# Pacing the convolution steps by a running account of VectorE's open work

## The chip, the cores and the metric

The kernel runs on one core of a Trainium2 chip. The metric is the device time of one execution in microseconds; of the kernel before, three runs took 519.13, 519.4 and 521.94 us, so the median is 519.4. The profile is of a further execution of 519.61 us, with a span of 517.8 us and a mean granted TensorE clock of 0.997.

## What is computed

The reference is a transformer block with adaptive layer norm: a gated long convolution over 2048 tokens, then a gated feed-forward layer. Cut to what matters, with D = 576 channels, S = 2048 tokens and F = 4608 hidden units:

```python
mod = silu(c) @ w_mod                      # six rows of D: sa, ca, ga, sb, cb, gb
h = layernorm(x) * (1 + ca) + sa
k_shift = causal_4_tap_filter(A_k, shift_k)
kv = k_shift * A_v
y = irfft(rfft(kv, 2 * S) * rfft(ssm_k, 2 * S))[:S] + kv * ssm_D   # causal convolution along tokens
x = x + ga * (h * y)
h = layernorm(x) * (1 + cb) + sb
out = x + gb * ((silu(h @ w1) * (h @ w3)) @ w2)
```

All inputs are bf16. The feed-forward layer of a token needs the convolution at that token, and the convolution at a token needs all tokens before it.

## The kernel before

**Two kinds of work.** The tokens are cut into 8 blocks of 256 for the convolution and into 4 row blocks of 512 (two blocks each) for the feed-forward layer. The feed-forward layer is nearly all TensorE work. The convolution is mostly VectorE work: for each block TensorE makes the spectra X (of kv) and W (of the filter) with small DFT matmuls, VectorE forms V from two neighbouring W, and then multiplies and adds a pair X[i], V[s-i] for every earlier block i (`pair`: products of 128 x 3456 elements, lines 414, 420, 422). VectorE makes the real parts (`real_parts`), TensorE transforms back (`inverse`, L554), VectorE gates the result and adds it to x (`residual`, L568 and L569), then the second layer norm follows and the rows are transposed on TensorE (L586) and evicted by ScalarE into h2T (L616), the operand of the feed-forward matmuls. Block 1's norm ends with L483 on VectorE; blocks 2 to 7 take sums on ScalarE (L452), then L458, L459 on VectorE, a power on GpSimd (L460), L466 on VectorE, and the rows on ScalarE (L581).

**How they are interleaved.** The convolution of the *next* row block runs beside the feed-forward layer of the present one. Block 0 is done alone at the start (`first_block`, to about 34 us). Row block 0 then starts with the tokens of block 0 alone (24 hidden chunks of 128, 256 tokens wide, two chunks to an item) while `conv_second` makes block 1; then come the tokens of block 1 for the same chunks and all 512 tokens for the rest, while `conv(2)` makes blocks 2 and 3. Row blocks 1 and 2 run beside `conv(4)` and `conv(6)`; row block 3 has no convolution beside it and its own loop (`stream_halves`).

A row block has two parts. `stream` computes silu(h w1) * (h w3): per item 16 or 8 full matmuls (L949) and a few over the last 64 channels (L960) into a PSUM tile of two banks, silu on ScalarE (L968), a copy of the other half on ScalarE (L970), and one product on VectorE (L971, called "product" below, 36 to a row block counting all 512 tokens). Products write `h3`. There are 4 PSUM tiles for everything, and 4 buffers for the copies. `down` then multiplies `h3` by w2 (L1061) in two halves of 288 columns, 144 matmuls each; after each half VectorE scales and adds the result (L1078, L1079). After the sixth of nine chunks of the second half, the program calls `end()` and `turn_all`, so that the transpose of the last block for the next row block stands there.

**What sets the order.** The convolution is written as generators. Each step lays out some instructions and yields a cost in microseconds of VectorE time. A negative yield says that the chain now waits for another engine for that long; `mix` fills such a wait with steps of a second generator, and if that has run out, it yields the wait as a positive cost. The feed-forward loops call `advance` after each item and after each down chunk, and `advance` lays out convolution steps. Before, `advance(cost)` adds a fixed amount to what is due and lays out steps until their costs have used it up. The amount is a rate times TensorE's time: 1.8 in the first stage (RATE1), then CONV_US of the row block over a stage time, times HEAD_PACE (1.8) for the first 8 items of row blocks 1 and 2; `conv(2)` starts with 12 us due. This is the order of layout; a scheduler of the layer underneath takes it as a priority and fixes the order in which the instructions of each engine are queued, by dependences and free buffers. Loads go through one queue, SyncE's, in its own order: weights for w1 and w3 into three buffers `wst` (two of them alternate in row blocks 1 to 3), w2 chunks, k and v rows, and the spectra of old blocks, which are spilled to DRAM and read back (`keep_x`, `keep_v`, `get`).

Of the kernel before, what the change touches and what calls it, by code (L numbers as in the profile page):

```python
# [26 lines left out]
NW13 = 3  # L27
W2C = 4
NW2 = 4
CONV_US = (72.0, 97.0, 108.0)  # L30
RATE1 = 1.8
FIRST_DUE = 12.0
N1 = 24
SPLIT = 2
HEAD = 8
HEAD_PACE = 1.8
EPS = 1e-5
EARLY_GETS = 6

# [7 lines left out]
class _Kernel:  # L47
    def __init__(self, ctx, tc, q, k, v, shift_k, ssm_k, ssm_D, w1, w3, w2, c, w_mod, out):
        self.tc, self.nc = tc, tc.nc
        self.q, self.k, self.v = q, k, v  # L50
        self.shift_k, self.ssm_k, self.ssm_D = shift_k, ssm_k, ssm_D
        self.w1, self.w3, self.w2, self.c, self.w_mod, self.out = w1, w3, w2, c, w_mod, out
        pool = lambda name, **kw: ctx.enter_context(tc.tile_pool(name=name, **kw))
        self.const = pool("const", bufs=1)
        self.psum = pool("psum", bufs=4, space=bass.MemoryType.PSUM)
        self.dram = pool("spill", bufs=1, space=bass.MemoryType.DRAM)
        self.spec = pool("spec", bufs=4)
        self.wprev = pool("wprev", bufs=2)
        self.prod = pool("prod", bufs=1)
        self.acc = pool("acc", bufs=1)  # L60
        self.ld = pool("ld", bufs=1)
        self.kvp = pool("kvp", bufs=1)
        self.x1p = pool("x1p", bufs=4)
        self.lnp = pool("lnp", bufs=1)
        self.small = pool("small", bufs=4)
        self.hp = pool("hp", bufs=4)
        self.xo, self.hg, self.accs, self.l1 = {}, {}, {}, {}
        self.X, self.V, self.Wl = {}, {}, {}
        self.w13, self.kept = {}, {}
        self.gets = 0  # L70

    def ps(self, shape=(P, 2, 512), dtype=F32):
        return self.psum.tile(list(shape), dtype, name="ps", tag="ps")
# [272 lines left out]
        yield 0.75  # L346

    def x_spectrum(self, s):
        X = self.spec.tile([P, 6, D], BF16, name="X", tag="X", bufs=3)
        self.X[s] = X  # L350
        if s < SPLIT:
            yield from self.forward(self.Fb, self.kv, lambda e, cs: X[:, 3 * e + 1 + cs, :])
        else:
            yield from self.forward2(self.Fb, self.kv, X[:, 1:3, :], X[:, 0:4:3, :], X[:, 4:6, :])

    def x_sums(self, s):
        X = self.X[s]
        self.nc.vector.tensor_add(X[:, 0:6:3, :], X[:, 1:6:3, :], X[:, 2:6:3, :])
        if 3 < s < NBLK - 2:
            self.keep_x(s)  # L360
        yield 0.75
# [538 lines left out]
            nc.sync.dma_start(t[:, 5 * i:5 * i + 4, :], w[0:512, cols].rearrange("(a p) f -> p a f", p=P))  # L900
            nc.sync.dma_start(t[64 * i:64 * i + 64, 4, :], w[512:D, cols])

    def advance(self, cost):

        self.due += cost
        while self.due > 0 and self.steps is not None:
            c = next(self.steps, None)
            if c is None:
                self.steps = None
                break  # L910
            self.due -= c
            self.spent += c

    def stream(self, r, jobs, rate, size, finish=False):

        nc = self.nc  # L920
        hT = self.h2T[r % 2]
        items = []
        for job in jobs:
            m = RB // (job[2] - job[1])
            items += [(job, fi, m) for fi in range(0, FC, m)]
        gus, ws = {}, {}

        def load(job):
            fc, _, _, buf, also = job
            if fc not in self.w13 and buf is not None:  # L930
                if r == 0:
                    with self.behind(nc.sync):
                        self.load_w13(fc, buf)
                else:
                    self.load_w13(fc, buf)
            w = self.kept[fc] = self.w13.pop(fc) if buf is not None else self.kept[fc]
            ws[job[0:3]] = w
            if also is not None:
                with self.behind(nc.sync):
                    also()  # L940


        def full(k, first):
            (fc, t0, t1, _, _), fi, m = items[k]
            w, n = ws[fc, t0, t1], t1 - t0
            for a in range(m):
                for i in range(2):
                    for ct in range(4):
                        nc.tensor.matmul(gus[k][:, i, a * n:(a + 1) * n],  # L949
                                         w[:, 5 * i + ct, (fi + a) * P:(fi + a + 1) * P], hT[:, ct, t0:t1],  # L950
                                         start=(first and ct == 0 and a == 0),
                                         stop=(not first and ct == 3 and a == m - 1))

        def rest(k, first):
            (fc, t0, t1, _, _), fi, m = items[k]
            w, n = ws[fc, t0, t1], t1 - t0
            for a in range(m):
                for i in range(2):
                    rows = slice(64 * i, 64 * i + 64)
                    nc.tensor.matmul(gus[k][:, i, a * n:(a + 1) * n],  # L960
                                     w[rows, 4, (fi + a) * P:(fi + a + 1) * P], hT[rows, 4, t0:t1],
                                     start=(first and a == 0), stop=(not first and a == m - 1))

        def hide(k):
            (fc, t0, t1, _, _), fi, m = items[k]
            f = fc * FC + fi
            h3 = self.h3[:, f:f + m, t0:t1]
            nc.scalar.activation(h3, gus[k][:, 0, :].rearrange("p (a t) -> p a t", a=m), ACT.Silu)  # L968
            u = self.hp.tile([P, RB], BF16, name="u", tag="u")
            nc.scalar.copy(u[:], gus[k][:, 1, :])  # L970
            nc.vector.tensor_mul(h3, h3, u[:].rearrange("p (a t) -> p a t", a=m))  # L971
            del gus[k]
            self.advance(rate * 2.05 * (HEAD_PACE if r > 0 and k < HEAD else 1.0))

        def begin(k):
            if items[k][1] == 0:
                load(items[k][0])
            gus[k] = self.ps()
        for k in range(0, len(items), size):
            early, late = range(k, k + size // 2), range(k + size // 2, k + size)  # L980
            for m in early:
                begin(m)
                full(m, True)
            for m in early:
                rest(m, False)
            for m in late:
                begin(m)
                rest(m, True)
            for m in early:
                hide(m)  # L990
            if finish and late.stop == len(items):
                self.end()
            for m in late:
                full(m, False)
                hide(m)
# [44 lines left out]
                part(f - 1, 1)  # L1040
                hide(f - 1)

    def down(self, r, rate):
        nc = self.nc
        for h in range(2):

# [3 lines left out]
            for f0 in range(0, NF, W2C):  # L1050
# [17 lines left out]
                if (f0 // W2C) % 4 == 3:  # L1068

                    leave = ((self.keep_v, 3), (self.keep_v, 2), (self.keep_x, 2), (self.keep_x, 3)) if r == 0 else ()  # L1070
                    for keep, i in leave[2 * h + f0 // (4 * W2C):][0:1]:
                        keep(i)
                self.advance(rate * W2C * 4 * 0.126)
            for t in range(4):
                s, cc = 2 * r + t // 2, t % 2
                x1 = self.xo[s]
# [7 lines left out]
                    nc.sync.dma_start(self.out[B * s:B * (s + 1), :].rearrange("(p c) d -> p c d", c=2),  # L1084
                                      x1[:])

    def begin(self, steps, due=0.0):
        self.steps, self.due, self.spent = steps, due, 0.0

    def end(self):  # L1090
        self.advance(1e9)

    def run(self):
        self.setup()
        self.early_loads()
        last = self.first_block()

        n1 = N1 // FC
        with self.tc.issue_after(last):
            self.begin(self.conv_second())  # L1100
            self.stream(0, [(fc, 0, 256, fc % 2, self.block_two if fc == n1 - 1 else None) for fc in range(n1)],
                        RATE1, 2, finish=True)
            self.end()
        sync = self.nc.sync.engine
        last = self.in_order(0, [sync])[sync]
        with self.tc.issue_after(last):
            self.row_blocks(n1)
# [6 lines left out]

    def row_blocks(self, n1):
        for r in range(NRB):
            cost = 0
            if r + 1 < NRB:
                s0 = 2 * r + 2

                self.begin(self.conv(s0), FIRST_DUE if r == 0 else 0.0)
                cost = CONV_US[r]
            time = 110.0 * 0.85 - (N1 * 1.03 if r == 0 else 0)
            rate = cost / time
            if r == 0:

                jobs = [(fc, 256, 512, None, None) for fc in (n1 - 2, n1 - 1)]
# [6 lines left out]
            else:  # L1134
                spills = {1: (self.keep_x, 1), 2: (self.keep_v, 0), 4: (self.keep_v, 1)} if r == 1 else {}
                jobs = [(fc, 0, RB, (r + fc) % 2, (lambda f, i: lambda: f(i))(*spills[fc]) if fc in spills else None)
                        for fc in range(NF // FC)]
            if r == NRB - 1:
                self.stream_halves(r)
            else:  # L1140
                self.stream(r, jobs, rate, 2)
            self.down(r, rate)
            self.end()


# [51 lines left out]
```

## Time and profile before

| quantity | value |
|---|---|
| median of 3 runs | 519.4 us |
| span of the profiled run | 517.8 us |
| TensorE matmul busy | 498.4 us (96%) |
| VectorE busy | 345.5 us (67%) |
| ScalarE busy | 292.9 us (57%) |
| products of spectra, L420 and L422 | 28 each, 54.6 us each |
| product of the stream, L971 | 108, 44.5 us |
| row block 0 starts (first L949) | 34.28 us |
| transpose of block 1 (L586) | 65.38 us |
| row block 1 starts | 171.45 us |
| row block 2 starts | 292.1 us |
| row block 3 starts | 408.57 us |

A row of the profile's groups names the source line, the engine, the operation, the tiles out and in, the shapes and the number of instructions, then the busy time and the mean duration of one, then the idle time of that engine just before them and what ended it. "PE" is TensorE's matmuls, "DVE" VectorE, "ACT" ScalarE, "POOL" GpSimd, "SP" SyncE. Busy time of TensorE includes pipelining, so two neighbouring matmuls overlap in the records; the time from the start of one to the start of the next is the better price. The slices give the busy share of each fortieth of the span in tenths.

### The profile page before, as it was taken

What the parts mean: (1) busy time and instruction counts of PE and PEld (TensorE: products, weight loads), DVE (VectorE), ACT (ScalarE), POOL (GpSimd) and SP (SyncE); (2) the same over time, 40 slices, a digit from 0 to 9 for tenths busy, and PEclk for the clock granted to TensorE, in tenths of its full rate; (3) what the DMA queues carried; (4) which work ended last, traced back from release to release, by engine and by line L of the source; (5) the groups of instructions that cost most, each with busy time, mean ns of one, the idle gap of its engine ahead of it and who ended that gap; (6) DMA issues with size and microseconds to landing.
All of it is one profiled execution on the core that took longest, in us unless ns stands there. A gap on an engine that the chain in (4) does not pass through costs nothing.

```text
span 517.8 us, 9255 instructions
## 1 busy us (share of the span) xinstructions
PE 498.4 (96%) x3650; PEld 294.8 (57%) x3650; DVE 345.5 (67%) x557; ACT 292.9 (57%) x581; POOL 26.1 (5%) x75
## 2 busy tenths in 40 slices
PE   7999989889989999899999999999999999999997
PEld 3667765456868544343677644434587644444775
DVE  8888799999997287989999637998711222221012
ACT  5748689649254488577641467958651355555000
POOL 3100000000000001000001000000100000000000
PEclk9999999989999999999999999999999999999999
DMA  8947959646998696688788549653655535532462
GB/s 262 331 151 210 308 178 289 203 143 221 315 342 270 207 312 230 214 284 289 230 270 280 161 147 361 200 173 91 184 147 151 161 107 176 175 110 77 117 181 69
DMA packets 102207, 107.80 MB, mean 208 GB/s; under 512 B 5075, under 2 KB 94228, under 8 KB 102164
## 3 DMA queue, kind: packets, MB, share of 16 engines
q1 hardware_dynamic: 102142, 107.21, 66.5%
q8 instruction: 28, 0.46, 0.4%
q14 instruction: 15, 0.12, 0.1%
q10 hardware_dynamic: 22, 0.01, 0.0%
HBM read 96.00 MB, written 11.21 MB: 207 GB/s over the span
## 4 chain that ended last, share of the span: by engine, by line
PE 70%; DVE 20%; DMA 4%; ACT 3%; issue 2%; POOL 1%; SPq 0%; DVEq 0%; POOLq 0%; ACTq 0%
PE ps L949 24%; PE ps L1061 22%; PE ps L1016 14%; PE ps L960 4%; DVE p L420 3%; DMA wst<-in_B_w_dram 3%; DVE z L422 3%; DVE h L971 2%; PE ps L318 2%; DVE z L414 1%; DVE kv L342 1%; DVE kvt L341 1%; PE ps L253 1%; DMA knat<-in_A_ssm_k_dram 1%; ACT junk L452 1%
## 5 line engine op out<-in xcount | busy, mean ns | idle before, releaser
L949 PE MATMUL ps<-h2T,wst 128*128 128x512 bf16 (+1 forms) x1056 | 201.1, 341 | 1.9 <-DMA wst<-in_B_w_dram 0.9
L949 PEld LDWEIGHTS <-wst 128*128 128x128 bf16 x1056 | 100.3, 98 | 87.7 <-issue 14.8
L1061 PE MATMUL ps<-wst,h 128*128 128x288 bf16 x1152 | 145.1, 286 | 2.4 <-DVE og L1078 1.4
L1061 PEld LDWEIGHTS <-h 128*128 128x128 bf16 x1152 | 112.3, 98 | 32.0 <-issue 3.1
L968 ACT ACTIVATE h<-ps 128x512 bf16<-128x512 f32 x108 | 65.2, 603 | 64.7 <-PE ps L960 40.8
L1016 PE MATMUL ps<-h2T,wst 64*128 64x512 bf16 x648 | 70.1, 376 | 0.0
L970 ACT CAST u<-ps 128x512 bf16<-128x512 f32 x108 | 63.7, 590 | 0.0
L971 DVE TENSOR_TENSOR h<-h,u 128x512 bf16<-128x512 bf16 x108 | 44.5, 417 | 24.6 <-ACT u L970 24.6
L420 DVE TENSOR_TENSOR p<-X,V 128x3456 bf16<-128x3456 bf16 x28 | 54.6, 1951 | 2.0 <-DMA X<-Xd 1.8
L422 DVE TENSOR_TENSOR z<-z,p 128x3456 bf16<-128x3456 bf16 x28 | 54.6, 1950 | 0.2
L1016 PEld LDWEIGHTS <-wst 64*128 64x128 bf16 x648 | 31.5, 94 | 38.4 <-DMA wst<-in_B_w_dram 0.4
L1031 DVE TENSOR_TENSOR h<-h,u 128x512 bf16<-128x512 bf16 x36 | 15.3, 425 | 54.9 <-ACT u L1030 54.9
L1078 DVE TENSOR_TENSOR og<-ps,gbrow 128x288 bf16<-128x288 f32 x32 | 13.1, 449 | 50.5 <-PE ps L1061 50.5
L1028 ACT ACTIVATE h<-ps 128x512 bf16<-128x512 f32 x36 | 21.5, 598 | 36.2 <-PE ps L1016 36.2
L452 ACT ACTIVATE junk<-x 128x576 bf16<-128x576 bf16 x54 | 37.1, 687 | 0.5
L616 ACT ACTIVATE h2T<-ps,sbcol,cbcol 128x256 bf16<-128x256 bf16 x35 | 16.7, 569 | 34.6 <-PE ps L586 34.6
L960 PE MATMUL ps<-h2T,wst 64*128 64x512 bf16 (+1 forms) x264 | 32.9, 341 | 0.0
L581 ACT ACTIVATE h2row<-x,l2n,l2r 128x576 bf16<-128x576 bf16 (+1 forms) x24 | 14.0, 660 | 13.4 <-DVE l2n L466 13.4
L1030 ACT CAST u<-ps 128x512 bf16<-128x512 f32 x36 | 20.9, 581 | 0.0
L960 PEld LDWEIGHTS <-wst 64*128 64x128 bf16 x264 | 8.5, 94 | 21.0 <-issue 19.9
L341 DVE TENSOR_TENSOR kvt<-kh,shk 128x1152 bf16<-128x1152 bf16 x24 | 18.1, 752 | 0.9 <-DMA kh<-in_A_k_dram 0.6
L342 DVE TENSOR_TENSOR kv<-kv,kvt 128x1152 bf16<-128x1152 bf16 x24 | 18.1, 754 | 0.4
(140 smaller groups left out, 389.5 us busy)
## 6 DMA issues: line engine op xcount, KB each, us to landing
wst<-in_B_w_dram SPq DMA_DIRECT2D x80, 512.0 KB, 4.3
wst<-in_B_w_dram SPq DMA_DIRECT2D x72, 288.0 KB, 3.6
X<-Xd SPq DMA_DIRECT2D x8, 864.0 KB, 7.1
Xd<-X SPq DMA_DIRECT2D x6, 864.0 KB, 5.2
wst<-in_B_w_dram SPq DMA_DIRECT2D x80, 64.0 KB, 3.3
kh<-in_A_k_dram SPq DMA_DIRECT2D x7, 720.0 KB, 6.4
Vd<-V SPq DMA_DIRECT2D x4, 864.0 KB, 8.1
V<-Vd SPq DMA_DIRECT2D x4, 864.0 KB, 6.4
```

What stands on the lines that cost most here:

```text
L341: nc.vector.tensor_mul(tmp[:], kh[:, 3 - j:5 - j, :], tap(j))
L342: nc.vector.tensor_add(kv[:], kv[:], tmp[:])
L420: nc.vector.tensor_mul(p[:], X[:], V[:])
L422: nc.vector.tensor_add(z[:], z[:], p[:])
L452: self.nc.scalar.activation(junk[:], src[:, i, :], func, scale=scale, accum_out=out[:, col:col + 1])
L949: nc.tensor.matmul(gus[k][:, i, a * n:(a + 1) * n], w[:, 5 * i + ct, (fi + a) * P:(fi + a + 1) * P], hT[:, ct, t0:t1], start=(first and ct ...
L960: nc.tensor.matmul(gus[k][:, i, a * n:(a + 1) * n], w[rows, 4, (fi + a) * P:(fi + a + 1) * P], hT[rows, 4, t0:t1], start=(first and a == 0 ...
L968: nc.scalar.activation(h3, gus[k][:, 0, :].rearrange("p (a t) -> p a t", a=m), ACT.Silu)
L970: nc.scalar.copy(u[:], gus[k][:, 1, :])
L971: nc.vector.tensor_mul(h3, h3, u[:].rearrange("p (a t) -> p a t", a=m))
L1016: nc.tensor.matmul(gus[f][:, i, :], w[rows, 5 * i + ct if ct < 4 else 4, cols], hT[rows, ct, :], start=swap == 0 and ct == 0, stop=swap == ...
L1061: nc.tensor.matmul(acc[t], self.h3[:, f0 + f, t * P:(t + 1) * P], w[:, f, :], start=(f0 + f == 0), stop=(f0 + f == NF - 1))
```

## The change

The fixed rates go, and with them CONV_US, RATE1, FIRST_DUE, HEAD and HEAD_PACE. In their place the program keeps, while it is laid out, an account of the work that VectorE has open (`backlog`): every item of the stream takes 2.05 us of TensorE time off it and adds 0.34 us for its own product, every down chunk takes 2.02 us off, and at the end of each half of `down` 2.5 us are added. While the account is below 3 us, convolution steps are laid out, and each adds 0.9 of its cost. At the start of `conv(4)` and `conv(6)` 8 us are taken off. `x_spectrum` first yields a wait of 2.5 us. The aim is that VectorE always has a little work queued, and never so much that the stream's products stand behind it. Which instructions there are does not change.

```diff
-CONV_US = (72.0, 97.0, 108.0)
-RATE1 = 1.8
-FIRST_DUE = 12.0
+AHEAD_US = 3.0
+SLIPPED_US = 8.0
 N1 = 24
 SPLIT = 2
-HEAD = 8
-HEAD_PACE = 1.8
...
     def x_spectrum(self, s):
+        yield -2.5
...
-    def advance(self, cost):
-
-        self.due += cost
-        while self.due > 0 and self.steps is not None:
+    def advance(self, time, vector=0.0):
+
+        self.backlog = max(self.backlog - time, min(self.backlog, 0.0)) + vector
+        while self.backlog < AHEAD_US and self.steps is not None:
             c = next(self.steps, None)
             if c is None:
                 self.steps = None
                 break
-            self.due -= c
-            self.spent += c
+            self.backlog += 0.9 * c
...
-            self.advance(rate * 2.05 * (HEAD_PACE if r > 0 and k < HEAD else 1.0))
+            self.advance(2.05, 0.34)
...
-                self.advance(rate * W2C * 4 * 0.126)
+                self.advance(W2C * 4 * 0.126)
+            self.backlog += 2.5
...
-    def begin(self, steps, due=0.0):
-        self.steps, self.due, self.spent = steps, due, 0.0
+    def begin(self, steps, slipped=0.0):
+        self.steps = steps
+        self.backlog -= slipped
 
     def end(self):
-        self.advance(1e9)
+        while self.steps is not None:
+            self.advance(1e9)
...
-                self.begin(self.conv(s0), FIRST_DUE if r == 0 else 0.0)
-                cost = CONV_US[r]
-            time = 110.0 * 0.85 - (N1 * 1.03 if r == 0 else 0)
-            rate = cost / time
+                self.begin(self.conv(2 * r + 2), SLIPPED_US if r > 0 else 0.0)
```

## The prediction

> **What bounds the kernel now.** I first read the busy shares and slices, then busy time by stage, then TensorE's gaps in order of time. Stages are cut at the first matmul (34.28), the transpose of block 1 (65.38), the first down matmul (130.2), and the starts of row blocks 1, 2 and 3 (171.45, 292.1, 408.57); line numbers are those of the kernel before.
>
> ```profile
> PE 498.4 (96%) x3650; PEld 294.8 (57%) x3650; DVE 345.5 (67%) x557; ACT 292.9 (57%) x581; POOL 26.1 (5%) x75
> ...
> DVE  8888799999997287989999637998711222221012
> ```
>
> TensorE is occupied nearly all the time, but slices 5 to 12 show VectorE full as well. The next table (stretch, its length, busy us with counts for PE, PEld, DVE, ACT, POOL, then clock, DMA share, GB/s) puts numbers on it.
>
> ```profile
> 34.28:65.38 31.10, 30.74 (x285) 23.60 (x284) 26.37 (x47) 22.45 (x44) 1.90 (x3) 1.00 0.72 225
> 65.38:130.20 64.82, 58.96 (x433) 36.17 (x431) 62.73 (x91) 50.34 (x104) 2.20 (x3) 0.97 0.67 208
> 130.20:171.45 41.25, 39.30 (x333) 31.14 (x332) 35.46 (x47) 15.73 (x31) 1.13 (x1) 1.00 0.92 293
> 171.45:249.80 78.35, 76.11 (x399) 31.75 (x397) 63.10 (x97) 58.07 (x116) 2.07 (x3) 1.00 0.81 265
> ```
>
> From 65 to 130 us VectorE is 97% busy; TensorE loses 5.9 us there, 2.0 us in the next stretch, and little elsewhere. Its gaps (start, length, matmul, idle before it and what ended it):
>
> ```profile
> 65.38 0.72 PE L586 MATMUL ps<-ident,h2row 128*128 128x128 bf16 x10
> 65.94 2.39 PE L949 MATMUL ps<-h2T,wst 128*128 128x256 bf16 x19
> 68.51 1.58 PE L949 MATMUL ps<-h2T,wst 128*128 128x256 bf16 x13 [0.19 <-ACT h2T L616]
> ...
> 105.56 1.12 PE L554 MATMUL ps<-z,Fb 128*128 128x288 bf16 x4 [3.72 <-DVE z L540]
> ...
> 154.72 10.45 PE L1061 MATMUL ps<-wst,h 128*128 128x288 bf16 x84 [1.41 <-DVE og L1078]
> 165.01 0.72 PE L586 MATMUL ps<-ident,h2row 128*128 128x128 bf16 x10
> 165.57 6.04 PE L1061 MATMUL ps<-wst,h 128*128 128x288 bf16 x48
> ```
>
> Two things matter. A transpose of a block (L586) is followed by its eviction to h2T on ScalarE (L616), and matmuls over those tokens can start 3.1 us after the transpose (65.38 to 68.51). And behind the transpose of block 3 at 165.01 stand 48 down matmuls, 6.04 us, which hide that eviction.
>
> How much is there to win? I add up TensorE's work at its unhindered pace: 0.222 us for a 512-wide matmul (16 in 3.56), 0.133 for a 64-row one, 0.1225 for 288 columns (16 in 1.96), 0.066 for a transpose. Row block 0 is 124.7 us of work and took 137.2 (34.28 to 171.45); row block 1 is 117.3 and took 120.6; row block 2 is 115.6 and took 116.5. A perfect pacing gains 12.5 + 3.3 + 0.9 = 16.7 us, no more.
>
> [...] at 101.8 TensorE stood 3.72 us before L554, with a full stream item behind it. [...] I read both built programs' orders. [...] the granted clock was 0.50 from 106 to 108 us after that gap, and work of 2.75 us took 4.26, 1.5 us lost. [...] the trace has 1.87 us from start to start for 3456 elements.
>
> **The change part by part.** No operation is added or removed; counts are equal on every engine. The fixed rates (1.8 in the first stage, head pace 1.8, 12 us of credit) go; `advance` hands out steps only while the counted backlog is under 3 us. Waits (the negative yields) that `mix` cannot fill come out positive and are counted as VectorE work though VectorE does nothing in them; that, and the extra 2.5 in `x_spectrum`, starves the early stage. The built order shows it (work ahead of an instruction on its own engine, from 34.05 on VectorE and 34.28 on TensorE; VectorE prices: 1.87 for 3456 elements, 0.67 for 1152, 0.34 for L971, 0.37 and 0.22 for L1078 and L1079):
>
> | ahead of | before | after |
> |---|---|---|
> | TensorE, last spectrum matmul of block 1 (L304) | 10.1 | 18.3 |
> | VectorE, last L483 of block 1 done | 24.4 | 32.2 |
> | TensorE, transpose of block 1 (L586) | 29.5 | 31.3 |
> | VectorE, product 36 (last L971 of row block 0) | 91.3 | 75.7 |
> | VectorE, last L466 of block 3 | 117.2 | 112.7 |
> | TensorE, transpose of block 3 | 118.2 | 124.0 |
>
> *Step 1, block 1.* VectorE now has products 4 to 8 in a row, then L358. Product 8 needs eight items on TensorE (17.3) and 1.1 on ScalarE; the spectrum needs two more L307 copies: 34.28 + 18.5 + 1.3 = 54.1. VectorE idles for it; its queue stood at 12.9. From there to the last L483 are 19.3 us of work, plus 0.7 for the two powers on GpSimd (0.32 and 0.52 before) and 0.6 for slower kv rows (0.79 apart at 140 us): 74.7, against 64.8 before. TensorE arrives at L586 at 34.28 + 31.3 = 65.6 and waits **9.1 us**; all that follows needs block 1's tokens, so it restarts at 74.7 + 3.1 = 77.8 with 31.9 us of work done: 11.6 us lost, against 1.9 at that place before. The idle exceeds the gap seen above: 1.5 us of half clock on top.
>
> *Step 2, blocks 2 and 3.* Products 15 to 20 stand in a row on VectorE; product 20 is ready at 34.28 + 11.6 + 1.5 + 49.6 + 1.1 = 98.1, where VectorE idles (it needs only 10.9 us for what lies between). From it to the last L466 of block 3 are 112.6 - 43.1 = 69.5 us: 167.6 if never idle. I count idles of 4.2 (products 24 to 27, one power), 4.4 (L458 of block 2 behind the sums on ScalarE; before, such a wait was up to 8.9) and 0.9 (a power, 0.71 plus its signals): **177.1**. What hides nothing: TensorE ends down at about 171.
>
> *Step 3, the transposes at the end.* No down matmul stands behind the transpose of block 3 now (48 before), so row block 1 starts at 177.1 + 3.3 (L466 to L586: 161.75 to 165.01) + 3.1 = 183.5, against 171.45: **+12.0**, and +1.5 of half clock. Bounds: with no idle in step 2, 174.0, +2.6 before the clock.
>
> *Step 4, row block 1.* After product 72, ready 79.2 us into the block, VectorE has 32.0 us to the last L466 plus 2 waiting for down's first half: 113.2, and the transpose needs 3 more; TensorE is there at 115.6. With 11 matmuls behind it the block takes about 118.6, against 120.6: **-2.0**.
>
> *Step 5, row block 2.* On VectorE two L1078 of down's second half now stand ahead of block 7's L466, so it can't come before down's end at 114.9; with the sums and the power 115.2, L581 2.6, transpose and eviction 2.7 more: about 120.5, against 116.5: **+4.0**.
>
> What costs nothing: earlier product and L1078 placements in row block 0 (TensorE waits elsewhere), and row block 3, whose order is unchanged. Sum: 12.0 + 1.5 - 2.0 + 4.0 = +15.5, **535 us**.
>
> **Rivals.** *Faster:* VectorE makes up the late start, since product 36 comes 15.6 us of work earlier; TensorE then never waits after 77.8. Row block 0 would end at 77.8 + 92.8 = 170.6, 0.9 sooner; with all of 3.3 + 0.9 in blocks 1 and 2, 514. The 97% share speaks for it, the runs of waiting products against. *No change:* step 1 is lost, step 2 idles not at all, steps 4 and 5 cancel: 519.4 + 2.6 = 522, or 520 if half of step 4's bound comes too. *Slower still:* loads of old spectra stand ahead of weight loads in the one SyncE queue and now wait for later VectorE work; before, such waits of TensorE were 0.9 and 0.4 us. Four such waits of 2.5 us: 545.
>
> **How the numbers follow.** My forecast 0.73, faster 0.07, no change 0.10, slower still 0.10. The range 522 to 545 takes in step 2's lower bound and the queue waits. Faster by over 0.5%: 0.07; within: 0.08; slower: 0.85.
>
> **What would show it.** In the changed profile: L586 of block 1 at about 75 with TensorE idle some 9 us before it and clock under 1 after; VectorE idle before products 5 to 8 and 15 to 20; the last transpose of row block 0 near 180 with no L1061 behind it; row block 3 starting about 15 us later than 408.57. Wrong if that first transpose comes before 68, or if VectorE's share in 65 to 130 stays at 97%.

## The result, and the profile after

The changed kernel takes **547.27 us** (median of four runs, 546.17 to 548.54), the kernel before, run beside it, 520.67 us (519.13 to 522.93). The ratio is 1.0508, with a 95% interval of 1.0456 to 1.056. The profiled span is 545.4 us against 517.8, 27.6 us longer, at a mean granted clock of 0.974 against 0.997. In what follows spans are compared with spans and medians with medians; a line number belongs to the kernel whose run is shown. In the changed kernel most lines stand one or two earlier than before: its stream matmul is L947, its down matmul L1059, its transpose L585, its product L969, and the last step of a norm on VectorE L465 (L466 before; some of the expectations below call it the last squares). The kernels of the experiments have more lines, so go by the tile names there.

From the page of the changed kernel, the busy times of the whole, then two rows of the 40 slices:

```profile
PE 507.5 (93%) x3650; PEld 304.3 (56%) x3650; DVE 347.8 (64%) x557; ACT 295.1 (54%) x581; POOL 26.3 (5%) x75
...
DVE  8884994669779966399799739849964312222011
...
PEclk9999969999999899999999999999999899999999
```

The counts are those of before and VectorE's busy time is 2.3 us more: nothing was added. VectorE's slices show where it went. Slices 6 to 12 were full before; now there are holes at slices 4 and 7 to 9, and full slices stand later. TensorE's busy time rose by 9.1 us with the same instructions; the lower clock in the last row (6 in slice 6, 8 in slices 14 and 32) goes with it, and the four slow restarts shown below add up to 8.0 us of it. The stages of row block 0 in the changed kernel, in the columns of the earlier table (cut at the first matmul, which comes at 33.73, the transpose of block 1, the first down matmul, and the start of row block 1):

```profile
33.73:75.67 41.94, 32.95 (x301) 25.05 (x299) 32.58 (x56) 24.77 (x48) 3.34 (x2) 0.97 0.59 188
75.67:136.86 61.19, 57.08 (x405) 34.26 (x405) 43.53 (x68) 39.85 (x80) 2.19 (x3) 0.94 0.66 204
136.86:188.77 51.91, 43.20 (x345) 33.22 (x343) 45.09 (x62) 23.09 (x47) 1.38 (x2) 0.94 0.82 261
```

(The 130.20 of the earlier table stands 0.3 us behind the first down matmul, which changes little.) The first stretch is 10.8 us longer than before, the middle one 3.6 us shorter and the last 10.7 us longer, though TensorE's busy time grows by only 2.2 us in the first and 3.9 us in the last. In the middle stretch VectorE's share is 43.53 / 61.19 = 71%, where it had been 97%. Part of its work was put off to the last stretch, which now holds 45.09 us of it, against 35.46 before. Summed over the program the row blocks give:

| | before | after | difference | forecast |
|---|---|---|---|---|
| row block 1 starts | 171.5 | 188.8 | +17.3 | +12.0 |
| row block 1 takes | 120.6 | 124.0 | +3.4 | -0.5 with the half clock |
| row block 2 takes | 116.5 | 121.0 | +4.5 | +4.0 |
| row block 3 and the end | 109.2 | 111.6 | +2.4 | 0 |

TensorE at the end of the first stage and at the end of row block 0, from its timeline (start, length, instruction; in brackets the idle time before it and what ended it):

```profile
75.67 0.71 PE L585 MATMUL ps<-ident,h2row 128*128 128x128 bf16 x5 [7.15 <-DVE l2mv L476]
77.14 0.72 PE L585 MATMUL ps<-ident,h2row 128*128 128x128 bf16 x5 [0.76 <-DVE h2row L482]
78.51 4.30 PE L947 MATMUL ps<-h2T,wst 128*128 128x256 bf16 x16 [0.65 <-ACT h2T L615]
...
148.11 0.64 PE L316 MATMUL ps<-kv,Fb 128*128 128x288 bf16 x2 [2.76 <-ACT X L318]
148.54 3.59 PE L1059 MATMUL ps<-wst,h 128*128 128x288 bf16 x16
...
186.31 0.71 PE L585 MATMUL ps<-ident,h2row 128*128 128x128 bf16 x5 [4.92 <-ACT h2row L580]
187.40 0.72 PE L585 MATMUL ps<-ident,h2row 128*128 128x128 bf16 x5 [0.38 <-ACT h2row L580]
188.77 3.66 PE L947 MATMUL ps<-h2T,wst 128*128 128x512 bf16 x8 [0.65 <-ACT h2T L615]
```

TensorE stands 7.15 us before block 1's transposes, restarts at 78.51, and does sixteen 256-wide matmuls in 4.30 us, which at full clock take 1.91 (at 100.54); the granted clock was 0.50 from 74 to 83 us and 1.00 from 100 to 103. The 2.76 us wait at 148.11 is followed by sixteen 288-column matmuls in 3.59 us, instead of 1.96, at a clock of 0.50 from 149 to 151. At the end TensorE has run out of down matmuls; it waits 4.92 us for block 3's rows, nothing stands behind the transposes, and the first eight matmuls of row block 1 take 3.66 us, at a clock of 0.50 from 186 to 192; at full clock eight take 1.89. Between the two ends VectorE waited in front of products (its timeline):

```profile
84.50 0.43 DVE L969 TENSOR_TENSOR h<-h,u 128x512 bf16<-128x512 bf16 x1 [2.29 <-ACT u L968]
...
95.00 0.42 DVE L969 TENSOR_TENSOR h<-h,u 128x512 bf16<-128x512 bf16 x1 [3.20 <-ACT u L968]
97.26 0.42 DVE L969 TENSOR_TENSOR h<-h,u 128x512 bf16<-128x512 bf16 x1 [1.84 <-ACT u L968]
99.34 0.42 DVE L969 TENSOR_TENSOR h<-h,u 128x512 bf16<-128x512 bf16 x1 [1.66 <-ACT u L968]
101.60 0.43 DVE L969 TENSOR_TENSOR h<-h,u 128x512 bf16<-128x512 bf16 x1 [1.84 <-ACT u L968]
```

With no convolution step between them the products arrive at TensorE's pace, 2.1 to 2.3 us apart, and VectorE idles 1.7 to 1.8 us of each. Row blocks 1 and 2 also end in a wait of TensorE for rows (2.12 us at 309.91, 2.05 us at 431.33). The end of row block 2, on TensorE, and below it the same place in the kernel before:

```profile
431.33 0.67 PE L585 MATMUL ps<-ident,h2row 128*128 128x128 bf16 x5 [2.05 <-ACT h2row L580]
432.42 0.71 PE L585 MATMUL ps<-ident,h2row 128*128 128x128 bf16 x5 [0.42 <-ACT h2row L580]
433.79 8.46 PE L1014 MATMUL ps<-h2T,wst 64*128 64x512 bf16 x56 [0.66 <-ACT h2T L615]
```

```profile
402.03 0.72 PE L586 MATMUL ps<-ident,h2row 128*128 128x128 bf16 x10
402.59 6.04 PE L1061 MATMUL ps<-wst,h 128*128 128x288 bf16 x48
408.57 6.65 PE L1016 MATMUL ps<-h2T,wst 64*128 64x512 bf16 x60
```

Before, 48 down matmuls stood behind that transpose and 60 of the first matmuls of row block 3 took 6.65 us, 0.111 each; now 56 take 8.46, at a clock of 0.50 from 432 to 438 us. The 2.2 us too much (8.46 - 56 x 0.111) are nearly the whole loss of the last row block, 2.4 us.

### The profile page after: what moved, and what is told of

Its sections match the earlier page's. It is cut to its first block, busy times and chain, and to the rows that moved or that the text cites. A ratio compares the mean times of both kernels' runs of the same rounds, so it can differ in the third digit from the quotient of the medians.

```text
span 545.4 us, 9261 instructions
## 1 busy us (share of the span) xinstructions
PE 507.5 (93%) x3650; PEld 304.3 (56%) x3650; DVE 347.8 (64%) x557; ACT 295.1 (54%) x581; POOL 26.3 (5%) x75
## 4 chain that ended last, share of the span: by engine, by line
PE 61%; DVE 21%; ACT 9%; DMA 5%; issue 3%; POOL 1%; SPq 1%; POOLq 0%; ACTq 0%; DVEq 0%
PE ps L947 22%; PE ps L1059 16%; PE ps L1014 13%; DVE p L419 4%; DVE z L421 4%; PE ps L958 4%; DMA wst<-in_B_w_dram 3%; ACT junk L451 2%; DVE kv L340 1%; PE ps L316 1%; DVE kvt L339 1%; DVE h L969 1%; DMA V<-Vd 1%; ACT hg L514 1%; ACT h2T L615 1%
## 5 line engine op out<-in xcount | busy, mean ns | idle before, releaser
L947 PE MATMUL ps<-h2T,wst 128*128 128x512 bf16 (+1 forms) x1056 | 204.6, 344 | 7.6 <-ACT u L968 3.1
L947 PEld LDWEIGHTS <-wst 128*128 128x128 bf16 x1056 | 100.8, 99 | 96.2 <-issue 21.3
L1059 PE MATMUL ps<-wst,h 128*128 128x288 bf16 x1152 | 147.4, 288 | 0.0
L1059 PEld LDWEIGHTS <-h 128*128 128x128 bf16 x1152 | 113.0, 98 | 30.0 <-issue 0.7
L969 DVE TENSOR_TENSOR h<-h,u 128x512 bf16<-128x512 bf16 x108 | 44.7, 418 | 45.4 <-ACT u L968 45.4
L1014 PE MATMUL ps<-h2T,wst 64*128 64x512 bf16 x648 | 72.5, 384 | 0.7 <-ACT h2T L615 0.7
L1014 PEld LDWEIGHTS <-wst 64*128 64x128 bf16 x648 | 39.2, 95 | 33.7 <-issue 1.8
L585 PE MATMUL ps<-ident,h2row 128*128 128x128 bf16 x70 | 7.5, 257 | 17.8 <-ACT h2row L580 9.9
L958 PEld LDWEIGHTS <-wst 64*128 64x128 bf16 x264 | 8.6, 95 | 21.8 <-issue 21.0
L372 ACT COPY kT<-ps 128x1152 bf16<-128x1152 bf16 x8 | 9.0, 1125 | 20.3 <-PE ps L370 20.3
```

The costliest lines, as they stand in the source:

```text
L947: nc.tensor.matmul(gus[k][:, i, a * n:(a + 1) * n], w[:, 5 * i + ct, (fi + a) * P:(fi + a + 1) * P], hT[:, ct, t0:t1], start=(first and ct ...
L958: nc.tensor.matmul(gus[k][:, i, a * n:(a + 1) * n], w[rows, 4, (fi + a) * P:(fi + a + 1) * P], hT[rows, 4, t0:t1], start=(first and a == 0 ...
L1014: nc.tensor.matmul(gus[f][:, i, :], w[rows, 5 * i + ct if ct < 4 else 4, cols], hT[rows, ct, :], start=swap == 0 and ct == 0, stop=swap == ...
L1059: nc.tensor.matmul(acc[t], self.h3[:, f0 + f, t * P:(t + 1) * P], w[:, f, :], start=(f0 + f == 0), stop=(f0 + f == NF - 1))
```

## The experiments

### The account in some stages, the old rate in the others

The kernels of this group hold both ways of pacing and choose by stage: block 1; blocks 2 and 3; blocks 4 and 5; blocks 6 and 7. Where a stage has the old rate, `x_spectrum` has no extra wait and the old constants apply.

```diff
+PACE = 'raaa'                    # first kernel; then 'arrr', 'rarr' and 'rraa'
...
-        yield -2.5
+        if PACE[s // 2] == 'a':
+            yield -2.5
...
-    def advance(self, time, vector=0.0):
+    def advance(self, time, vector=0.0, head=1.0):
+        if PACE[self.stage] == 'a':
             self.backlog = max(self.backlog - time, min(self.backlog, 0.0)) + vector
...
+            return
+        if self.stage == 0:
+            rate = RATE1
+        else:
+            r = self.stage - 1
+            rate = CONV_US[r] / (110.0 * 0.85 - (N1 * 1.03 if r == 0 else 0))
+        self.due += rate * time * head
+        while self.due > 0 and self.steps is not None:
...
```

*The old rate in the first stage alone.*

> The changed kernel with block 1's convolution (the first stage) paced by the old rate 1.8 again, the account from there on. Theory A, each stage loses by its own late steps and the stages overlap: block 1's transpose back at about 65, product 20 ready at 87, and from there the 83.6 us that the changed kernel needed to the last L466 of block 3, so row block 1 starts near 174; the rest as in the changed kernel (+3.4, +4.6, +2.4): 13 over before, about 534. Rival B, the first stage is no loss of its own because VectorE's total work to block 3 sets the end of row block 0: no more than 3 us below the changed kernel, about 544. Rival C, all of the loss is the late start of block 1: as before, about 521.

*The account in the first stage alone.*

> The kernel before with only the first stage paced by the account (and the 2.5 us wait ahead of block 1's spectrum). Theory A: block 1's transpose at 75 to 77 as in the changed kernel, but VectorE is then full to block 3 (84.9 us of work and some 3 idle from 77.3): last L466 of block 3 near 165, row block 1 starts near 176; nothing more is lost after: +4 to +5, about 525. Rival B: 0 to +1, 521. Rival C: nearly the whole loss, 545.

*The account for blocks 2 and 3 alone.*

> The kernel before with only the convolution of blocks 2 and 3 paced by the account. Theory A: block 1's transpose at 65, row block 1 starts near 174 with a cold TensorE: +3 to +5, about 525. Rival B (VectorE's total sets the end; it idles while products are waited for): +10 or more, 531. Rival C: 521.

*The account for blocks 4 to 7 alone.*

> The kernel before with only the convolutions of blocks 4 to 7 (beside row blocks 1 and 2) paced by the account. Theory A: row block 1 starts at 171.5 as before; row block 1 gains or loses up to 2, the transposes of blocks 5 and 7 come with no down matmuls behind them, row block 2 loses 4.6 and row block 3 starts cold, 2.4: +7 to +9, about 529. Rival B: as theory A. Rival C: 521.

Measured, with row block lengths from each trace:

| account in | median us | ratio and interval | row block 1 starts | 1 | 2 | 3 |
|---|---|---|---|---|---|---|
| nowhere (before) | 519.68 | 1 | 171.5 | 120.6 | 116.5 | 109.2 |
| all but block 1 | 534.59 | 1.027 (1.0237 to 1.0303) | 176.7 | 124.1 | 120.9 | 111.4 |
| block 1 | 529.81 | 1.0175 (1.0145 to 1.0206) | 180.8 | 120.7 | 116.5 | 109.3 |
| blocks 2, 3 | 524.75 | 1.0098 (1.0058 to 1.0137) | 174.8 | 122.1 | 116.5 | 109.6 |
| blocks 4 to 7 | 532.67 | 1.0235 (1.0201 to 1.0269) | 170.7 | 125.0 | 122.7 | 111.6 |

The three parts cost 10.1, 5.1 and 13.0 us, 28.2 in sum, and the whole change 26.6: they very nearly add up, so there is no single culprit. Two of the forecasts held (534, and 525 for blocks 2 and 3); two were too low (525 for block 1, 529 for blocks 4 to 7). Behind the account in block 1 the stages with the old rate are as long as before, so the mixed kernels do pace them as before. The first stage was dearer than expected, because VectorE's late start was not made up at all: the last norm step of block 3 came at 170.93 instead of 161.59, with the old rate all the way from block 2. The last part was the largest and the most underrated. In it row block 0 is that of before, and row blocks 1 to 3 are still as long as in the changed kernel or longer: what goes wrong in row block 1 does therefore not need a late start. (One thing differs: here the account begins row block 1 some 2.5 us fuller than in the changed kernel, since the stage with the old rate does not work off what the first half of down added. That may be why its row blocks 1 and 2 are a little longer.) A cold restart adds to it: with the account in blocks 2 and 3 alone, whose first eight matmuls of row block 1 take 3.56 us, not 1.89, that row block is 1.5 us longer than before.

### What starves it: the added wait, the charged waits, the limit

Four versions with the account in all stages, each with one thing changed, and the last with two. `Wait` marks the waits that `mix` could not fill.

```diff
-        yield -2.5                      # first version: without the added wait
...
-                    yield -c            # in mix; second and fourth version
+                    yield Wait(-c)
...
-            self.backlog += 0.9 * c
+            self.backlog += 0.0 if isinstance(c, Wait) else 0.9 * c
...
-AHEAD_US = 3.0
+AHEAD_US = 18.0                         # third version; 9.0 in the fourth
```

*Without the added wait of 2.5 us.*

> The changed kernel without the added wait of 2.5 us at the head of each spectrum. Theory W, what starves VectorE is that waits which nothing fills are booked as VectorE's work, all of them, not this one: the built order keeps block 1's spectrum (18.3) and its last L483 (32.2) where they were, so within 3 us of the changed kernel, about 546. Rival D, the added wait is what delays the spectra: 530 or less.

541.03 us, ratio 1.0422 (1.0366 to 1.0478), between the two forecasts. Block 1's transpose still comes at 75.7, after an idle of 6.85 us. The added wait costs some 5 to 6 us of the 27 (the intervals of the two ratios just overlap), and is not what starves the first stage.

*Waits that could not be filled cost nothing in the account.*

> The changed kernel, but a wait that nothing fills adds nothing to the account (it is laid out as before, at no cost). Theory W: block 1 stays late (last L483 still behind 32.2 us of VectorE work, transposes near 75, row block 1 near 176), but down matmuls stand behind the transposes of blocks 3, 5 and 7 again (48 each) and VectorE has 107.7 instead of 112.6 us ahead of block 3's last L466: the losses of row blocks 1 to 3 go, about 523. Rival E, the limit of 3 us is too small whatever is booked: within 5 us of the changed kernel, 542 to 547.

537.95 us, 1.0358 (1.0313 to 1.0403): a miss. It gives back 8 to 9 us (row block 1 starts at 183.9 and takes 122.3), not 24. The 48 down matmuls stand behind the transposes of blocks 3, 5 and 7 again, as forecast, and row block 3 takes 109.8; but row block 1 was to start at 176. Block 1's transpose is not earlier (76.9, after 6.20 us of idle). In the prediction the charge for waits, with the added wait, starves the first stage; neither does it by itself.

*A limit of 18 us in place of 3.*

> The changed kernel with 18 us in place of 3 as the limit of the account; waits are booked as in the changed kernel. Both theories W and E: the larger limit covers the booked waits; last L483 of block 1 behind 24.1 us of VectorE work as before the change, last L466 of block 3 behind 121.6 (117.1 before the change), 24 down matmuls behind its transpose instead of 48: row block 1 at 176, later blocks as before the change, about 525. If the losses were something else than late steps (the weights' queue, say): 540 or more.

534.18 us, 1.0271 (1.023 to 1.0312): a miss. Block 1's transpose comes at 69.2, so the limit does matter there, but row block 0 ends only 5 us sooner than with 3 us (183.4). TensorE now waits for the kv rows that VectorE makes:

```profile
84.03 0.66 PE L323 MATMUL ps<-kv,Fb 128*128 128x288 bf16 x2 [5.53 <-DVE kv L349]
```

Steps laid out earlier carry their matmuls with them: behind these two stand 16 matmuls of the stream, which start at 84.48 with no wait of their own and take 3.10 us instead of 1.91. In row block 0 TensorE also waits 6.9 us in sum for weights, against 2.9 us in the changed kernel.

*Both: free waits and a limit of 9.*

> Both: unfilled waits cost nothing in the account, and its limit is 9 us. Theory W: block 1's last L483 behind 24.4 us of work as before the change, its transposes at 65; product 36 behind 80.5 (91 before the change) and block 3's last L466 behind 109.5 (117.1); 48 down matmuls behind the transposes of blocks 3, 5 and 7. TensorE is then the bound to product 36 (about 122), the last L466 comes near 157, row block 1 starts near 166: about 511, faster than both. Rival F, VectorE's saturation sets the end of row block 0 whatever the order: row block 1 at 171, about 519.

527.36 us, 1.0146 (1.0111 to 1.0182): row block 1 starts at 172.8, close to the old 171.5, with 48 down matmuls behind block 3's transpose again. What remains is mainly row block 1 (125.1). I had expected 511; nothing came of the 12 us that TensorE loses in row block 0 before. A new loss takes half of them: TensorE waits 6.3 us for weights in row block 0, where it waited 0.5 us before. What held the loads up I did not take apart.

### The half clock after the first wait

> The changed kernel with 28 extra 512-wide matmuls on TensorE, their result unused, just ahead of block 1's transposes, where TensorE stands idle for 7.15 us. They add no wait and fill about 6 us of that gap (28 x 0.215 us at full clock, about twice that in part if cold), so TensorE should still be at full clock when the first row block restarts at 78.5. Theory C (the slow matmuls after the wait are a clock loss of about 2.4 us that is carried to the end): the restart's sixteen 256-wide matmuls take about 1.8 us rather than 4.3 and the whole takes 544.5 to 545.5 us. Rival (VectorE, not TensorE, sets the end of this stretch, so that a warm start only lengthens the next wait for VectorE): 547 us, with the six waits before L969 longer by the 2.4 us in sum.

```diff
+        with self.behind(self.nc.tensor):
+            self.warm(28, self.shk[:, 0, 0:512])   # 28 matmuls, result unused
         self.turn_all(1)
```

549.85 us, 1.0573 (1.0519 to 1.0628), with runs from 546.98 to 552.53. TensorE in that kernel, and then its stretches of 1 us with the granted clock as third number from the right:

```profile
68.38 6.20 PE L648 MATMUL ps<-shk,ident 128*128 128x512 bf16 x28
75.73 0.50 PE L593 MATMUL ps<-ident,h2row 128*128 128x128 bf16 x5 [1.14 <-DVE l2mv L484]
77.54 0.52 PE L593 MATMUL ps<-ident,h2row 128*128 128x128 bf16 x5 [1.31 <-DVE h2row L490]
...
78.72 4.30 PE L970 MATMUL ps<-h2T,wst 128*128 128x256 bf16 x16 [0.44 <-ACT h2T L623]
```

```profile
76.00:77.00 1.00, 0.23 (x4) 0.09 (x1) 0.61 (x1) 0.00 (x0) 1.00 (x1) 1.00 0.00 0
77.00:78.00 1.00, 0.46 (x6) 0.47 (x7) 0.95 (x3) 0.00 (x0) 0.01 (x1) 0.89 0.00 0
78.00:79.00 1.00, 0.56 (x3) 0.11 (x2) 0.96 (x2) 0.90 (x2) 0.00 (x0) 0.50 0.00 0
```

The 28 matmuls ran at full clock (6.20 us, 0.22 each; in the kernel before eight took 0.215 each, from 220.05 to 221.77), and the transposes after them too (0.50 us for five, against 0.71). But in the 3.3 us from 74.6, with two waits over 1 us and two groups of transposes, TensorE was busy less than a third of the time, and the clock fell all the same, just before the stream restarted. So the experiment did not take away what it was meant to take away, and whether a warm restart would be carried to the end is left open by it. What it does show is that filling the long wait wasn't enough here: the clock was lost in the chain of the transposes.

### The lateness of the last two stages

> The account for blocks 4 to 7 only, old rates before, with 20 us instead of 8 us taken off the open work at the start of each of the last stages, so that the convolution's steps of row blocks 1 and 2 start earlier among the products (52 and 55 us of VectorE work were in the products' windows with 8 us, 68 and 61 in the kernel before). With 8 us it was 532.7 us. Theory L (the loss of that part is lateness: the last squares of blocks 5 and 7 come after the down product's matmuls have run out, TensorE idles 2 to 2.6 us, restarts cold): row block 1 back to about 121.5, row block 2 to 117.5 to 119 (block 7's squares still have two rows of the down product's output ahead of them), row block 3 to 109.5; the whole 522 to 525 us. Rival O (the account's bunching of steps costs it, not how late they start): within 2 us of 532.

```diff
-SLIPPED_US = 8.0
+SLIPPED_US = 20.0                # with PACE = 'rraa'
```

525.45 us, 1.0104 (1.0062 to 1.0146), against 532.67 with 8 us and just above the 522 to 525 forecast. The profiled run, at 527.21, is the slowest of its four. First the two parts of row block 1 (stream, then down) with 8 us taken off, then with 20; VectorE is the third busy time:

```profile
170.70:249.70 79.00, 78.31 (x403) 32.41 (x402) 51.75 (x87) 56.49 (x113) 2.07 (x3) 1.00 0.69 220
249.70:295.70 46.00, 40.38 (x336) 31.77 (x335) 42.36 (x56) 16.31 (x32) 2.33 (x1) 0.97 0.75 232
```

```profile
174.20:255.00 80.80, 79.56 (x414) 33.10 (x412) 64.19 (x100) 58.61 (x118) 3.63 (x3) 1.00 0.75 244
255.00:294.80 39.80, 39.04 (x329) 30.92 (x326) 36.76 (x41) 15.44 (x31) 0.69 (x1) 1.00 0.81 254
```

With 8 us VectorE had only 51.75 us of work beside the stream and 42.36 beside down, where it is 92% busy and TensorE, with 40.38 us of work in 46, waits 2.59 us for block 5's rows at 293.22. Another 2.01 us of its idle time, at 259.75, is a wait for weights (0.70 us with 20). With 20 us, 12 us of VectorE's work go back beside the stream, down has 48 matmuls behind the transpose again, and row block 1 takes 120.6 instead of 125.0. That part of the theory held: lateness was the loss of row block 1, but for the 1.3 us that the weights may be. Row block 2 kept 121.4 of its 122.7, where 117.5 to 119 was expected. Part of that is the transposes, which still wait 1.44 us at 409.92; its stream took 82.2 us, against 79.0 in the kernel before, with three waits of 0.57 to 0.93 us for ScalarE's copies late in it; I did not take these apart.

### Blocks 2 and 3 with free waits and a limit of 9; the account from there on

> The account for blocks 2 and 3 only (row block 0), old rates elsewhere, with the waits charged at nothing and a limit of 9 us in place of 3 us. With the account as the change has it in that part the whole took 524.75. Theory: the account is not wrong in itself; where it lets steps run ahead of VectorE by more and charges no unfilled wait, the last squares of block 3 come before the old order's, 48 of the down product's matmuls or more are left behind its transposes, and the whole takes 517 to 521 us, no more than before. Rival: spectra that come early hold TensorE up at VectorE's and ScalarE's products, as at 150 and 250 us with the account everywhere (527.4): 523 us or more.

```diff
+PACE = 'rarr'                    # and AHEAD_US = 9.0, Wait as above
```

518.68 us (median of 20 runs, 517.62 to 520.01), beside 519.95 of before (23 runs); ratio **0.9976** (0.9964 to 0.9987). Against 1.0098 of the same part with the limit of 3 and charged waits, the two edits win 6 us. The end of row block 0 on TensorE:

```profile
162.25 0.72 PE L597 MATMUL ps<-ident,h2row 128*128 128x128 bf16 x10
163.37 4.08 PE L1084 MATMUL ps<-wst,h 128*128 128x288 bf16 x32 [0.40 <-DMA wst<-in_B_w_dram]
167.81 2.12 PE L1084 MATMUL ps<-wst,h 128*128 128x288 bf16 x16 [0.36 <-DMA wst<-in_B_w_dram]
169.77 1.89 PE L972 MATMUL ps<-h2T,wst 128*128 128x512 bf16 x8
```

The transposes no longer wait, 48 matmuls hide their eviction, and the first eight of row block 1 run at full clock (1.89 us). In this stage an account is thus not worse than a rate. The gain is only a quarter of a per cent, though the interval leaves out 1. The 1.3 us are a small part of the 12.5 that row block 0 could give: a wait of 2.74 us for ScalarE's copies at 94.67 takes the place of the 3.72 us that TensorE lost at 101.8 before. It is the one version that is faster than both kernels.

> Old rate in the first stage alone; the account from block 2 on with waits charged at nothing, a limit of 9 us and 20 us taken off at the start of each of the last two stages. It is the version of the account that the runs so far point to. If lateness and the unfilled waits are the whole of what the account lost after the first stage: 518 to 522 us. If steps that come early make TensorE wait for VectorE's and ScalarE's products inside row block 1 (two waits of 1.6 and 1.2 us at 252 and 254 with the limit of 9): 524 to 528.

```diff
+PACE = 'raaa'                    # and AHEAD_US = 9.0, SLIPPED_US = 20.0, Wait as above
```

527.92 us, 1.0132 (1.0095 to 1.017): the second of the two outcomes. Row block 1 starts at 169.3, but takes **132.2** us in the profiled run, which at 531.87 us is the slowest of the five; the others may have lost less. TensorE in it:

```profile
188.28 3.24 PE L972 MATMUL ps<-h2T,wst 128*128 128x512 bf16 x8 [1.90 <-ACT u L993]
...
241.55 0.66 PE L565 MATMUL ps<-z,Fb 128*128 128x288 bf16 x4 [1.13 <-DVE z L551]
...
244.09 1.14 PE L565 MATMUL ps<-z,Fb 128*128 128x288 bf16 x4 [1.66 <-DVE z L552]
...
247.53 3.16 PE L972 MATMUL ps<-h2T,wst 128*128 128x512 bf16 x8
```

This is the other side of the optimum. The early steps fill VectorE (20.00 of 20 us busy from 230 to 250), the inverse's matmuls stand in TensorE's queue before VectorE has made z, and the stream waits behind them: its eight matmuls at 247.53 have no wait of their own. After two waits of 1.13 and 1.66 us, 2.5 us apart, the clock is 0.66 in the mean from 242 to 246 us and 0.50 from 246 to 250, and those eight take 3.16 us. That is about half of the loss. Most of the other half begins at ScalarE: TensorE waits for its copies 0.57 us at 180.84, 0.17 at 185.98 and 1.90 at 188.28, and the eight matmuls behind the last wait take 3.24 us.

## Where the prediction was right, and which steps failed

The direction was right, and so was the mechanism of row block 0: late convolution steps in the first stage, products waiting in a row on VectorE, and transposes with nothing behind them. The size was not: 15.5 us forecast, 27.6 in the span, and 547 lies beyond the range. Three terms failed. Step 2 brought the end of row block 0 too early (5.3 us, net of step 3), step 4 gave row block 1 a gain where it lost (3.9 us with its clock), and row block 3 was put at nothing (2.4 us). By its own steps:

*What starves the first stage: not the two causes named.* The prediction blamed the waits charged as work and the added 2.5 us. Without the charge block 1's transposes come at 76.89, without the added wait at 75.71, against 75.67. A limit of 18 us alone brings them to 69.15. So the limit of 3 us holds the steps back there, with or without either of them; a version without both and with that limit was not run.

*Step 1, block 1: right in its times.* Transpose at 75.67 (74.7 forecast), restart at 78.51 (77.8). The idle was 7.15 us instead of 9.1, as TensorE had itself come 2.9 us later, in part because of two waits for weights (1.27 us at 44.34, 0.37 us at 49.02). The half clock cost about 2.4 us here, not 1.5.

*Step 2, VectorE to the last norm step of block 3: too small.* Products 15 to 20 wait in a row as forecast, but product 20 came at 101.60 and not at 98.1. The norm step came at 185.19, 8.1 us later than 177.1:

```profile
185.19 0.16 DVE L465 TENSOR_TENSOR l2n<-l2s,l2r 128x2 f32<-128x2 f32 x1 [0.50 <-POOL l2r L459]
```

From product 20 to it are 83.6 us, for which I had 69.5 of work and 9.5 of idle. In the trace VectorE is busy for 72.05 us of them and idle for 11.5: some 2.6 us of work and 2.0 us of waits were missing. The price of the work is one reason: the 1152-element steps at 171.52, 172.32 and 173.11, each of which uses a tile of the one before (kv or kvt), start 0.80 and 0.79 us apart; 0.67, the distance between the steps at 178.03, 178.70 and 179.37, had been charged for all.

*Step 3, the end of row block 0: the absence of down matmuls was right, the chain was charged too much.* From the norm step to the stream's restart were 3.6 us (185.19 to 188.77), not 6.4. The 3.3 us taken for the first part of it come from the kernel before, where TensorE was at down matmuls without a break until the transposes at 165.01; here it stands idle, and the first half's transposes start 1.1 us after the norm step, while ScalarE still makes the rows of the second. Hence 188.8 instead of 183.5: 8.1 us of later norm less 2.8. The half clock after it was 1.8 us, near the 1.5 charged.

*Step 4, row block 1: the step that failed in sign.* I gave it -2.0 (118.6 us) and it takes 124.0. The last product of the stream was to come 79.2 us into the block and came at 85.0 (273.81); even in the kernel before it had come at 86.0. Down starts 82.2 us in, after the cold start, a wait of 1.82 us at 262.56 for ScalarE's copy, and others, and the product then needs 2.8 us more. From it to the last norm step are 35.0 us, near my 34.0. So that step comes 120.0 us in, not 113.2, and the 2.12 us wait at 309.91 is that. The account in blocks 4 to 7 alone, with a row block 0 as before, still has 125.0, so a loss of this size belongs to the stage itself. It divides otherwise there: the product comes at 81.9 and the norm step 39.6 us after it, at 121.4. Starting the steps earlier brings 120.6. I had compared the order of VectorE's queue with TensorE's and found enough room, which was true for work without waits.

*Step 5, row block 2: right in size by luck.* It takes 121.0, for 120.5. The forecast had two L1078 of the last down result hold up block 7's norm step. They do not: the trace has the inverse on TensorE and then, on VectorE, the residual and the norm step.

```profile
421.55 1.14 PE L553 MATMUL ps<-z,Fb 128*128 128x288 bf16 x8
...
423.45 0.76 DVE L567 TENSOR_TENSOR hg<-hg,y 128x1152 bf16<-128x1152 bf16 x1 [8.48 <-ACT y L759]
...
430.22 0.16 DVE L465 TENSOR_TENSOR l2n<-l2s,l2r 128x2 f32<-128x2 f32 x1 [0.50 <-POOL l2r L459]
```

VectorE had z ready at 415.0, but the inverse stood in TensorE's queue behind down matmuls (137 from 404.77, 16.95 us) until 421.55, 108.8 us into the block (83.0 before). VectorE waits 8.48 us for its result, then ScalarE's sums follow, and the norm step comes at 430.22.

*What I took to cost nothing: wrong for row block 3.* Its order is unchanged, but it starts after an idle of 2.05 us and further small ones, and its first matmuls cost 2.2 us of clock. I charged the clock only after idles of 3.7 us and more; it also fell after this one (0.71 from 431 to 432 us, then 0.50).

Together: 5.3 us from step 2 less step 3, 3.9 from step 4 with its clock, 0.5 from step 5 and 2.4 from row block 3 are the 12.1 that were missing. *The rival "slower still"*, four waits for weights of 2.5 us each, gave nearly the time that came, but for a reason that isn't there: the three such waits in row block 0 sum to 2.9 us, the longest 1.3. *"VectorE makes up the late start"* is refuted by the account in the first stage alone, where block 1's transposes come 9.7 us late and row block 1 starts 9.3 us late, with the old rates in between.

## What to carry to other kernels

When the order of two queues decides, count in both the work and the waits: a new pacing shifts steps in each stage, and here every stage lost on its own (10, 5 and 13 us). An account of open work must not be so short that the steps come when the stream has run out (here the limit of 3 us), and counting as work what is only waiting makes it shorter still. Steps too early cost as well, since their matmuls stand in front of the stream in TensorE's queue (5.53 us at once with the limit of 18). Whatever the pacing, look first at whether a block's transposes still have matmuls behind them, because that one place cost the wait, the eviction and then the clock (at the end of row block 0 4.92 us, 2.46 from the first transpose to the restart, and 1.8).

## What the runs showed of the hardware

The clock was lost after shorter idles than I had reckoned with, which was from the one gap of 3.72 us in the kernel before. In the changed kernel a single idle of 2.76 us (148.11), and in the account for blocks 4 to 7 with 20 us taken off one of 2.00 us (below), were followed by half clock for some 3 us and cost 1.6 to 1.7 us each; in the last kernel above a pair of 1.13 and 1.66 us was followed by half clock for about 6 us. At the ends of stages, with their several waits, the first matmuls after the restart lost 1.8 to 2.4 us. Two kernels with the same order at this place, the first wait for VectorE in down of row block 0, are the account in blocks 4 to 7 with 8 us taken off, and then the one with 20:

```profile
153.93 10.45 PE L1080 MATMUL ps<-wst,h 128*128 128x288 bf16 x84 [1.81 <-DVE og L1098]
```

```profile
155.79 12.12 PE L1080 MATMUL ps<-wst,h 128*128 128x288 bf16 x84 [2.00 <-DVE og L1098]
```

The same 84 matmuls take 10.45 us after an idle of 1.81 and 12.12 us after one of 2.00; the clock was 1.00 throughout in the first, and 0.50 from 157 to 159 us in the second. This pair alone could be a threshold between 1.81 and 2.00 us. A second pair rules that out: the account for blocks 2 and 3 with free waits and a limit of 9, and the last kernel above, which has the same order up to here.

```profile
94.67 3.22 PE L972 MATMUL ps<-h2T,wst 128*128 128x512 bf16 x8 [2.74 <-ACT u L993]
```

```profile
94.74 1.89 PE L972 MATMUL ps<-h2T,wst 128*128 128x512 bf16 x8 [2.74 <-ACT u L993]
```

After the same idle of 2.74 us the eight matmuls take 3.22 us in the first and 1.89 us, the full-clock time, in the second. In the changed kernel, too, the clock was 1.00 from 309 to 315 us, after the idle of 2.12 us at 309.91, and fell after the 2.05 us at 431.33. So in these runs, for idles of 1.81 to 2.76 us, the length of a single idle did not decide whether the clock fell; what did, no trace here shows.

The prediction takes the queue of every engine in its built order. For TensorE the traces show places where that held: matmuls that waited 3.72 us (105.56 in the kernel before) and 5.53 us (84.03 with the limit of 18) had matmuls of the stream behind them (107.81 and 84.48), which then had no wait of their own. For VectorE and ScalarE it was my estimate.
